# First two blocks of an attention and MLP kernel: scores from keys in place, value tiles loaded, weights decoded in four single steps, a new prologue order

## The chip, the cores and the metric

The kernel runs on one core of one Trainium2 chip. The metric is the device time of one execution in microseconds (us). Five engines work side by side, each with its own queue in order: TensorE (PE; its weight loads are listed as PEld), VectorE (DVE), ScalarE (ACT), GpSimd (POOL) and SyncE (SP), which issues all transfers here.

## The reference

`B, H, S, D = 4, 8, 768, 64`; the model width is 512, the MLP width 1536.

```python
k_sum = k.reshape(B, H, nb, block, D).max(axis=3)      # block = 32
v_sum = v.reshape(B, H, nb, block, D).mean(axis=3)
mask_l = np.abs(pos[:, None] - pos[None, :]) < window  # window = 16
scores_l = scale * q @ k^T, -1e9 outside mask_l
scores_s = scale * q @ k_sum^T + log(block)
a = softmax(concat([scores_l, scores_s]))
x = a @ concat([v, v_sum])                             # then heads side by side
g = x @ w_gate;  out = (silu(g) * (x @ w_val)) @ w_out
```

Each position sees its neighbours within 16 and 24 pooled blocks. The MLP weights arrive as float64.

## The kernel before

The 3072 tokens are 8 blocks of 384, two per batch. A block's attention runs by four pairs of heads u; a pair has 128 partitions (two heads of 64). Queries come in six tiles of 64; a tile's keys are a window of 96 and 24 pooled ones, so a score row has 120 columns. The MLP runs by 12 steps j of 128 hidden units; every product is made of three in a short float format, from a high and a low part of each operand. A step of one block is three groups on PE: gate (12 matmuls), val (12) and down (9 of 512 columns, accumulated in three banks over all j).

Every weight is decoded once on the chip, from the two 32-bit words of a float64: ACT takes the absolute value of the high word into a tile `m` (`w_abs`); DVE clamps it (L183), shifts it (L185), sets sign and top bits (L193) and the bits of the low word (L196); a cast makes the high part (`w_hi`, L152 on DVE or L150 on ACT) and a subtraction the low part (`w_lo`, L146 on DVE or POOL). Gate and value weights of steps 1 to 10 go together as `gv` (1024 columns, "wide"), those of steps 0 and 11 and all output weights `o` have 512 ("narrow"). Step 11 is loaded only when the pool `dec`, which holds the `m` tiles of `gv`, is closed (`room(1)`).

The first two blocks (k = 0 and 1) are a prologue: a hand-held table, `PROLOGUE`, lists every step in the order in which it is issued, with the engine behind `=` (`a` ACT, `d` DVE, `p` POOL) where there is a choice. Each engine keeps that order. The table ends with block 0 complete and with steps 0 to 5 of block 1: 18 steps, 54 groups. From there a loop issues the rest of the MLP, with the attention of later blocks between. Names of the table: `kt` and `q` load keys and queries; `winA`, `winB`, `join` put block 0's windows together out of `kt` and the pooled keys; `kw` loads windows for block 1; `pool` makes the pooled keys; `scores`; `ttr` adds bias and takes the maximum; `exp`; `rcp` the reciprocal of the sum; `nrm` multiplies by it; `tr` and `pt` transpose and copy from PSUM; `out` multiplies by the values; `split` and `rest` make high and low part of x; `silu`, `mul`, `ah`, `al` make the high and low part of the MLP's middle. Argument pairs are (block, pair) up to `rest` and (block, step) behind it.

Block 0's values: `vn` loads value rows in tiles of 128 starting at 0, from which windows of even query tiles are read in place; `odd1`, `odd2` copy odd windows out of it, `first_values` sums blocks on PE, `fv_copy`, `val1`, `val2` copy these sums behind each window. Block 1's windows are loaded by `vw` and completed by `values`.

SP issues in order and has eight transfer semaphores, so an issue waits for the eighth before it.

Of the kernel before, what the change touches and what calls it, by code (L numbers as in the profile page):

```python
# [72 lines left out]
fv_copy(0)=a nrm(0,1)=d tr0(0,3) pt1(0,3)=a w_load(1,gv) pt0(0,3)=a val1(0,1)=d tr1(0,1) val2(0,1)=a pool(2)
join(0,0)=p tr0(0,1) val1(0,2)=p pt1(0,1)=a out(0,3) winB(0)=p w_abs(0,g) winA(2)=d join(0,2)=d pt0(0,1)=a
w_clamp(0,g) val1(0,0)=a out(0,1) vw(1,0) split(0,3)=a w_bits(0,g) winB(2)=a vw(1,1) val2(0,0)=a scores(1,0)
split(0,1)=a rest(0,3) q(0,0) rest(0,1) w_abs(1,gv) w_load(0,v) w_hi(0,g)=d ttr0(1,0) w_lo(0,g)=p values(1,0)=a
ttr1(1,0) w_load(2,o) exp0(1,0) values(1,1)=p scores(0,0) w_clamp(1,gv) w_load(0,o) exp1(1,0) ttr0(0,0)
w_abs(0,v) w_load(1,o) rcp(1,0) exp0(0,0) ttr1(0,0) nrm(1,0)=p q(0,2) exp1(0,0) w_load(3,o) w_clamp(0,v)
tr1(1,0) tr0(1,0) pt1(1,0)=a rcp(0,0) scores(1,1) w_bits(0,v) w_abs(2,o) w_load(2,gv) w_abs(1,o) scores(0,2)
ttr0(1,1) nrm(0,0)=p w_abs(0,o) pt0(1,0)=a ttr1(1,1) exp0(1,1) out(1,0) w_clamp(1,o) kw(1,3) w_clamp(0,o)  # L80
tr0(0,0) exp1(1,1) tr1(0,0) ttr0(0,2) kw(1,2) pt1(0,0)=a rcp(1,1) q(1,2) split(1,0)=a ttr1(0,2) nrm(1,1)=p
pt0(0,0)=a vw(1,2) rest(1,0) exp0(0,2) out(0,0) w_load(4,gv) w_bits(0,o) exp1(0,2) tr0(1,1) tr1(1,1) join(1,2)=d
w_hi(0,v)=d join(1,3)=a scores(1,2) rcp(0,2) pt0(1,1)=a values(1,2)=d pt1(1,1)=a nrm(0,2)=d w_load(5,gv)
w_hi(0,o)=a out(1,1) split(0,0)=a w_bits(1,o) tr1(0,2) split(1,1)=a tr0(0,2) pt1(0,2)=a rest(0,0) w_lo(0,v)=p
pt0(0,2)=a ttr0(1,2) w_hi(1,o)=a out(0,2) vw(1,3) rest(1,1) w_lo(0,o)=p exp0(1,2) ttr1(1,2) q(1,3) split(0,2)=d
room(0) w_load(7,gv) exp1(1,2) w_lo(1,o)=p rest(0,2) gate(0,0) rcp(1,2) values(1,3)=d nrm(1,2)=d val(0,0)
silu(0,0) w_bits(1,gv) w_load(6,gv) tr1(1,2) tr0(1,2) pt1(1,2)=a scores(1,3) w_clamp(2,o) w_hi(1,gv)=a
w_load(9,o) mul(0,0) pt0(1,2)=a w_lo(1,gv)=p ttr0(1,3) ah(0,0)=a out(1,2) ttr1(1,3) exp0(1,3) w_load(8,o)
split(1,2)=d rest(1,2) w_load(7,o) gate(0,1) w_bits(2,o) exp1(1,3) w_load(9,gv) al(0,0)=d w_abs(2,gv) rcp(1,3)
val(0,1) nrm(1,3)=d silu(0,1) w_clamp(2,gv) w_load(8,gv) tr1(1,3) w_bits(2,gv) tr0(1,3) w_abs(6,gv) down(0,0)  # L90
pt1(1,3)=a pt0(1,3)=a w_hi(2,o)=a w_clamp(6,gv) out(1,3) w_load(6,o) w_hi(2,gv)=a mul(0,1) w_lo(2,gv)=p
split(1,3)=a w_load(3,gv) ah(0,1)=a rest(1,3) gate(1,0) val(1,0) silu(1,0) al(0,1)=d w_abs(4,gv) w_bits(6,gv)
w_load(10,o) down(0,1) w_load(5,o) mul(1,0) w_lo(2,o)=d ah(1,0)=a w_load(10,gv) al(1,0)=d gate(1,1) w_abs(7,o)
w_hi(6,gv)=d w_abs(3,o) w_clamp(7,o) w_abs(6,o) w_clamp(3,o) val(1,1) silu(1,1) w_bits(7,o) w_load(4,o)
w_lo(6,gv)=d w_hi(7,o)=a down(1,0) w_clamp(6,o) w_abs(3,gv) mul(1,1) w_lo(7,o)=p ah(1,1)=a gate(0,2) al(1,1)=d
w_abs(4,o) w_clamp(3,gv) w_bits(6,o) val(0,2) silu(0,2) w_bits(3,gv) w_hi(6,o)=a down(1,1) mul(0,2) w_hi(3,gv)=d
gate(1,2) ah(0,2)=d w_lo(3,gv)=d al(0,2)=d val(1,2) w_lo(6,o)=d silu(1,2) w_clamp(4,o) w_bits(3,o) down(0,2)
mul(1,2) w_hi(3,o)=a w_clamp(4,gv) ah(1,2)=a gate(0,3) al(1,2)=d w_bits(4,gv) val(0,3) silu(0,3) w_bits(4,o)
w_hi(4,gv)=d w_hi(4,o)=a down(1,2) mul(0,3) w_lo(3,o)=p ah(0,3)=d w_abs(8,o) w_lo(4,gv)=d gate(1,3) w_abs(9,o)
al(0,3)=d w_abs(7,gv) w_clamp(9,o) w_abs(5,gv) w_clamp(8,o) val(1,3) w_bits(9,o) silu(1,3) w_clamp(5,gv)  # L100
down(0,3) mul(1,3) w_clamp(7,gv) ah(1,3)=a gate(0,4) al(1,3)=d w_bits(7,gv) val(0,4) silu(0,4) w_bits(8,o)
down(1,3) mul(0,4) w_hi(8,o)=a w_hi(7,gv)=d ah(0,4)=a w_lo(4,o)=d al(0,4)=d w_abs(10,o) gate(1,4) w_bits(5,gv)
val(1,4) silu(1,4) w_clamp(10,o) w_hi(5,gv)=d w_bits(10,o) down(0,4) w_lo(5,gv)=d w_hi(10,o)=d gate(0,5)
mul(1,4) w_lo(8,o)=p ah(1,4)=a al(1,4)=d w_abs(5,o) w_hi(9,o)=d val(0,5) w_clamp(5,o) silu(0,5) w_lo(10,o)=p
w_bits(5,o) down(1,4) mul(0,5) w_lo(9,o)=p gate(1,5) w_hi(5,o)=d ah(0,5)=d w_lo(5,o)=d al(0,5)=d w_lo(7,gv)=p
val(1,5) silu(1,5) down(0,5) mul(1,5) w_abs(8,gv) ah(1,5)=a w_clamp(8,gv) w_abs(10,gv) gate(0,6) al(1,5)=d
w_bits(8,gv) val(0,6) silu(0,6) w_clamp(10,gv) down(1,5) w_hi(8,gv)=d w_bits(10,gv) gate(0,7) mul(0,6)
w_lo(8,gv)=p ah(0,6)=a val(0,7) silu(0,7) al(0,6)=d w_abs(9,gv) w_hi(10,gv)=d down(0,6) mul(0,7) w_clamp(9,gv)
ah(0,7)=d w_lo(10,gv)=d gate(0,8) al(0,7)=d w_bits(9,gv) val(0,8) silu(0,8) w_hi(9,gv)=d down(0,7) mul(0,8)
w_lo(9,gv)=d ah(0,8)=a al(0,8)=p room(1) w_load(11,g) gate(0,9) w_load(11,v) val(0,9) silu(0,9) w_load(11,o)  # L110
w_abs(11,g) w_clamp(11,g) down(0,8) mul(0,9) w_abs(11,v) w_bits(11,g) ah(0,9)=a w_abs(11,o) gate(0,10) al(0,9)=d
w_hi(11,g)=d w_clamp(11,o) w_clamp(11,v) val(0,10) silu(0,10) w_bits(11,o) w_bits(11,v) w_hi(11,o)=a down(0,9)
# [13 lines left out]
def body(ctx, tc, qP, kP, vT, vP, wgv, wo, bias, ident, mean, out):  # L126
# [51 lines left out]
    def w_clamp(j, nm):  # L178

        low, high, m = W[nm, j]  # L180
        f = m.bitcast(I32)

        nc.vector.tensor_scalar(out=m, in0=m, scalar1=F64_LO, scalar2=F64_HI, op0=ALU.max, op1=ALU.min)  # L183

        nc.vector.tensor_scalar(  # L185
            out=f, in0=f, scalar1=3, scalar2=0x3FFFFFF8,
            op0=ALU.logical_shift_left, op1=ALU.bitwise_and,
        )

    def w_bits(j, nm):  # L190
        low, high, m = W[nm, j]
        f = m.bitcast(I32)
        nc.vector.scalar_tensor_tensor(  # L193
            out=f, in0=high, scalar=-0x40000000, in1=f, op0=ALU.bitwise_and, op1=ALU.bitwise_or
        )
        nc.vector.scalar_tensor_tensor(  # L196
            out=f, in0=low, scalar=29, in1=f, op0=ALU.logical_shift_right, op1=ALU.bitwise_or
        )
# [531 lines left out]
```

## Time and profile before

| | |
|---|---|
| median of 3 runs | 736.31 us (736.21 to 736.46) |
| span of the profiled execution | 735.9 us, the profiled execution's own time by its records |
| PE busy | 707.3 us (96%), 4958 matmuls |
| DVE busy | 302.2 us (41%) |
| ACT busy | 310.3 us (42%) |
| POOL busy | 156.6 us (21%) |
| moved by DMA | 62.02 MB, mean 84 GB/s |

The shares are means over two unlike stages: the prologue, in which attention and all weights are prepared, and the long stage behind it. A profile row gives start, duration, engine, line, operation, output and inputs; a bracket gives the idle time ahead and what ended it. A group row gives busy time and mean duration of one in ns.

### The profile page before, as it was taken

The numbers are of one execution on the slowest core, as the hardware profiler recorded it, in microseconds if no ns is written. First come the engines' busy times: TensorE is split into PE (matmuls) and PEld (weight loads), VectorE is DVE, ScalarE is ACT, GpSimd is POOL, SyncE is SP. The second block draws the span as 40 slices with busy tenths as digits, with TensorE's granted clock in tenths as the row PEclk, the third lists the DMA queues.
The fourth block names the chain that finished last, engine by engine and source line by source line (L and its number), as shares of the span: only waits on it lengthen the run. The fifth ranks groups of instructions, "written<-read, shape, count | busy, mean of one in ns | idle before, by whom it ended". The sixth has DMA issues, their size and how long they took to land.

```text
span 735.9 us, 12480 instructions
## 1 busy us (share of the span) xinstructions
PE 707.3 (96%) x4958; PEld 643.5 (87%) x4958; DVE 302.2 (41%) x833; ACT 310.3 (42%) x772; POOL 156.6 (21%) x161
## 2 busy tenths in 40 slices
...
GB/s 311 320 307 413 94 1 0 1 73 97 208 155 167 65 44 45 30 79 65 69 85 87 109 38 7 44 86 44 44 44 44 54 33 17 1 14 31 1 0 44
DMA packets 56666, 62.02 MB, mean 84 GB/s; under 512 B 24288, under 2 KB 46752, under 8 KB 55328
## 3 DMA queue, kind: packets, MB, share of 16 engines
...
## 4 chain that ended last, share of the span: by engine, by line
PE 80%; DVE 10%; issue 3%; ACT 3%; DMA 2%; POOL 1%; SPq 0%; DVEq 0%; POOLq 0%; ACTq 0%
PE v L494 24%; PE g L494 24%; PE acc L545 23%; PE xo L468 3%; PE sc L378 3%; PE pp L444 2%; DVE m_gv L193 1%; DMA stg<-in_kP 1%; PE pv L359 1%; ACT p L408 1%; DVE w_gv L146 1%; DVE a L506 1%; DVE m_gv L196 1%; DMA bias_sb<-in_bias 1%; DVE m_gv L185 1%
## 5 line engine op out<-in xcount | busy, mean ns | idle before, releaser
L494 PE MATMUL g<-xh,w_gv 128*128 128x384 f32 x640 | 179.8, 342 | 5.6 <-DVE w_gv L146 4.4
L494 PE MATMUL v<-xh,w_gv 128*128 128x384 f32 x640 | 180.0, 342 | 1.4 <-DVE a L506 1.4
L545 PE MATMUL acc<-w_o,ah 128*128 128x512 f32 x576 | 179.2, 392 | 0.0
L506 DVE TENSOR_TENSOR a<-v,a 128x384 f32<-128x384 f32 x96 | 53.4, 556 | 248.7 <-PE v L494 248.0
L146 POOL TENSOR_TENSOR al<-a,ah 128x384 fp32r<-128x384 f32 x79 | 80.7, 1022 | 270.2 <-ACT ah L150 260.1
L494 PEld LDWEIGHTS g<-xh,w_gv 128*128 128x128 f32 x640 | 118.4, 190 | 9.0 <-issue 4.4
L545 PEld LDWEIGHTS acc<-w_o,ah 128*128 128x128 f32 x576 | 108.0, 188 | 20.2
L494 PEld LDWEIGHTS v<-xh,w_gv 128*128 128x128 f32 x640 | 117.9, 189 | 5.0 <-issue 2.4
L545 PE MATMUL acc<-w_o,al 128*128 128x512 f32 x288 | 114.1, 396 | 0.1
L501 ACT ACTIVATE a<-g 128x384 f32<-128x384 f32 x96 | 47.2, 492 | 156.5 <-PE g L494 152.5
L494 PE MATMUL g<-xl,w_gv 128*128 128x384 f32 x320 | 108.8, 340 | 0.0
L494 PE MATMUL v<-xl,w_gv 128*128 128x384 f32 x320 | 108.1, 338 | 0.0
L150 ACT CAST ah<-a 128x384 fp32r<-128x384 f32 x91 | 46.4, 510 | 126.0 <-DVE a L506 126.0
L408 ACT ACTIVATE p<-p,nm 128x120 f32<-128x120 f32 x192 | 73.2, 383 | 2.5 <-DVE nm L393 2.1
L545 PEld LDWEIGHTS acc<-w_o,al 128*128 128x128 f32 x288 | 54.0, 188 | 10.2 <-issue 0.6
L494 PEld LDWEIGHTS g<-xl,w_gv 128*128 128x128 f32 x320 | 60.7, 190 | 2.5
L494 PEld LDWEIGHTS v<-xl,w_gv 128*128 128x128 f32 x320 | 60.5, 189 | 0.0
L430 POOL TENSOR_TENSOR p<-p,ri 128x720 f32<-128x720 f32 x27 | 37.8, 1401 | 101.8 <-DVE ri L426 95.7
L501 ACT ACT_TABLE_LOAD x26 | 33.4, 1283 | 52.3 <-PE g L494 52.2
L393 DVE CUSTOM_DVE_ANT_0 p<-sc,bias_sb 128x120 f32<-128x120 f32 x192 | 41.4, 276 | 2.2 <-PE sc L378 2.0
L494 PE MATMUL g<-xh,w_g 128*128 128x384 f32 x128 | 37.5, 355 | 0.0
L494 PE MATMUL v<-xh,w_v 128*128 128x384 f32 x128 | 36.3, 344 | 0.0
...
## 6 DMA issues: line engine op xcount, KB each, us to landing
...
kw<-in_kP SPq DMA_DIRECT2D x28, 288.0 KB, 4.0
vw<-in_vP SPq DMA_DIRECT2D x28, 288.0 KB, 3.3
...
out<-o SPq DMA_DIRECT2D x23, 256.0 KB, 2.3
...
```

Of the source, the lines that this page charges most:

```text
L146: (nc.vector if e == "d" else nc.gpsimd).tensor_tensor(out=out, in0=a, in1=b.bitcast(F32), op=ALU.subtract)
L150: nc.scalar.copy(out, in_)
L378: nc.tensor.matmul(sc[h][s * QT : (s + 1) * QT, c * KC : (c + 1) * KC], t["q"][hs, qs], t["kw"][hs, i, :], start=True, stop=True,)
L393: nc.vector.tensor_tensor_reduce(out=t["p"][:, i, :], in0=t["sc"][g][:, c * KC : (c + 1) * KC], in1=bias_sb[:, 0 if n == 0 else 2 if n == ...
L408: nc.scalar.activation(out=t["p"][:, i, :], in_=t["p"][:, i, :], func=AF.Exp, scale=-1.0, bias=t["nm"][:, i : i + 1], accum_out=t["sm"][:, ...
L430: (nc.vector if on == "d" else nc.gpsimd).tensor_tensor(out=p, in0=p, in1=ri.rearrange("p (n o) -> p n o", o=1).broadcast_to([P, NT, KC]), ...
L444: nc.tensor.transpose(ps[:KC, c * P : (c + 1) * P], U[k, u]["p"][:, g * NT // 2 + c, :], id_sb)
L468: nc.tensor.matmul(ps[hs, qs], vw, t["pt"][:, h, qs], start=True, stop=True)
L494: nc.tensor.matmul(ps[:, :TOK], w[:, cs], x, start=u == 0 and n == 0, stop=u == NP - 1 and n == 2)
L501: nc.scalar.activation(out=a, in_=A.pop(("g", k, j))[:, :TOK], func=AF.Silu)
L506: nc.vector.tensor_tensor(out=a, in0=ps[:, :TOK], in1=a, op=ALU.mult)
L545: nc.tensor.matmul(ACC[k][i], a[:, ts], w, start=j == 0 and n == 0, stop=j == NJ - 1 and n == 2)
```

## The change

Scores of blocks 0 and 1 are made in two parts: `sw` multiplies a query tile with 96 columns of the key tile in place, `sp` with the 24 pooled keys. No windows are copied, joined or loaded in these blocks. Even and odd value windows of both blocks come from two tiles, `vn` (all four pairs, loaded by `vn` and `vr`) and `vo` (loaded by `vo`, from row 64 on). The block sums of all pairs land in one bank (`fv`), four copies move them out (`fvc`), and two transfers from on-chip memory to on-chip memory spread them behind all even and all odd windows (`spn`, `spo`). The decoding steps of a weight, `w_clamp` (two instructions) and `w_bits` (two), become `w_c1`, `w_c2`, `w_s1`, `w_s2`, each with its own place in the table. PSUM banks are named in the table (`g`, `a`, `b`). Gate and val of step 0 can be issued by pair (`gate(0,0,2)`). The table is new as a whole.

```diff
+    def a_score_part(k, u, keys, cols):
+        t = U[k, u]
+        for i in range(NT):
+            c, s = divmod(i, 2)
+            qs = slice(i * QT, (i + 1) * QT)
+            for h in range(2):
+                hs = slice(h * D, (h + 1) * D)
+                nc.tensor.matmul(
+                    t["sc"][h][s * QT : (s + 1) * QT, c * KC + cols[0] : c * KC + cols[1]], t["q"][hs, qs],
+                    keys(hs, i), start=True, stop=True,
+                )
+    def a_near(k, u):
+        U[k, u]["sc"] = [a_bank(k, u, f"sc{h}", on[h]) for h in range(2)]
+        a = k % HALVES * TOK
+        a_score_part(k, u, lambda hs, i: KT[u][hs, a + i * QT : a + i * QT + KW], (0, KW))
+    def a_far(k, u):
+        a_score_part(k, u, lambda hs, i: ksum[u][hs, :], (KW, KC))
...
+    def v_sums():
+        vn["sums"] = ps = a_bank(0, 0, "pv", on)
+        for i in range(NV):
+            for u in range(NP):
+                nc.tensor.matmul(
+                    ps[u * QC : (u + 1) * QC, :P], mean_sb[:, i, :], vn["even"][:, i, u * P : (u + 1) * P],
+                    start=i == 0, stop=i == NV - 1,
+                )
+    def v_keep():
+        vsum["all"] = one.tile([KC, DM], F32, tag="vs", name="vs_0")
+        ps = vn.pop("sums")
+        for u in range(NP):
+            copy(on, vsum["all"][KW:, u * P : (u + 1) * P], ps[u * QC : u * QC + NB, :P])
+    def v_spread(x):
+        src = vsum["all"][KW:].rearrange("n (o d) -> n o d", o=1).broadcast_to([NB, ODD, DM])
+        nc.sync.dma_start(vn[x][KW:KC, :ODD], src)
...
-                if k:
-                    vw = t["vw"][:, i, hs]
-                else:
-                    vw = t["vw"][:, i // 2, hs] if i % 2 else t["vn"][:KC, i // 2, hs]
+                if k < HALVES:
+                    w = k * NT + i
+                    vw = vn["odd" if w % 2 else "even"][:KC, w // 2, u * P + h * D : u * P + (h + 1) * D]
...
-q(0,3) kt(3) kt(1) q(0,1) mean() bias() pool(3) winB(3)=p vn(2) winA(3)=p join(0,3)=a winA(1)=d winB(1)=a
+kt(0) q(0,0) pool(0) bias() sw(0,0)=ag sp(0,0) q(1,0) ttr0(0,0) mean() sw(1,0)=aa sp(1,0) kt(1) ttr1(0,0)
```

POOL, from the first wide subtraction on, before (`w_gv1` is the pair of tiles of step 1; `al_0_8` belongs to block 0, step 8):

```order
L146 TENSOR_TENSOR w_gv1_753<-m_gv1_354,w_gv1_753 128x1024
L146 TENSOR_TENSOR w_gv2_888<-m_gv2_818,w_gv2_888 128x1024
L146 TENSOR_TENSOR w_o7_1000<-m_o7_968,w_o7_1000 128x512
L146 TENSOR_TENSOR w_o3_1122<-m_o3_972,w_o3_1122 128x512
L146 TENSOR_TENSOR w_o8_1284<-m_o8_1179,w_o8_1284 128x512
L146 TENSOR_TENSOR w_o10_1341<-m_o10_1293,w_o10_1341 128x512
L146 TENSOR_TENSOR w_o9_1364<-m_o9_1195,w_o9_1364 128x512
L146 TENSOR_TENSOR w_gv7_1286<-m_gv7_1199,w_gv7_1286 128x1024
L146 TENSOR_TENSOR w_gv8_1494<-m_gv8_1443,w_gv8_1494 128x1024
L146 TENSOR_TENSOR al_0_8_1598<-a_0_8_1581,ah_0_8_1596 128x384
```

and after, from the first MLP step on:

```order
L147 TENSOR_TENSOR al_0_0_856<-a_0_0_832,ah_0_0_854 128x384
L147 TENSOR_TENSOR w_o0_849<-m_o0_717,w_o0_849 128x512
L147 TENSOR_TENSOR al_1_0_954<-a_1_0_893,ah_1_0_946 128x384
L147 TENSOR_TENSOR al_0_1_1015<-a_0_1_959,ah_0_1_998 128x384
L147 TENSOR_TENSOR al_1_1_1068<-a_1_1_961,ah_1_1_1066 128x384
L147 TENSOR_TENSOR w_gv3_1116<-m_gv3_951,w_gv3_1116 128x1024
L147 TENSOR_TENSOR w_gv5_1108<-m_gv5_1033,w_gv5_1108 128x1024
L147 TENSOR_TENSOR w_o3_1178<-m_o3_1090,w_o3_1178 128x512
L147 TENSOR_TENSOR al_1_2_1220<-a_1_2_1071,ah_1_2_1161 128x384
L147 TENSOR_TENSOR w_gv4_1217<-m_gv4_1156,w_gv4_1217 128x1024
```

The subtractions `al`, which stood on DVE before, now stand on POOL between the weights, and six wide `w_lo` are there instead of four.

DVE, in the middle of the weights, before:

```order
L183 TENSOR_SCALAR m_o7_968<-m_o7_968 128x512
L185 TENSOR_SCALAR m_o7_968<-m_o7_968 128x512
L183 TENSOR_SCALAR m_o3_972<-m_o3_972 128x512
L185 TENSOR_SCALAR m_o3_972<-m_o3_972 128x512
L193 SCALAR_TENSOR_TENSOR m_o7_968<-raw_o7_794,m_o7_968 128x512
L196 SCALAR_TENSOR_TENSOR m_o7_968<-raw_o7_794,m_o7_968 128x512
L146 TENSOR_TENSOR w_gv6_970<-m_gv6_852,w_gv6_970 128x1024
```

and after, at the weights of steps 3 to 5:

```order
L185 TENSOR_SCALAR m_gv3_951<-m_gv3_951 128x1024
L147 TENSOR_TENSOR w_o1_996<-m_o1_779,w_o1_996 128x512
L181 TENSOR_SCALAR m_gv5_1033<-m_gv5_1033 128x1024
L185 TENSOR_SCALAR m_gv5_1033<-m_gv5_1033 128x1024
L193 SCALAR_TENSOR_TENSOR m_gv5_1033<-raw_gv5_798,m_gv5_1033 128x1024
L193 SCALAR_TENSOR_TENSOR m_gv3_951<-raw_gv3_928,m_gv3_951 128x1024
L200 SCALAR_TENSOR_TENSOR m_gv3_951<-raw_gv3_928,m_gv3_951 128x1024
L181 TENSOR_SCALAR m_o3_1090<-m_o3_1090 128x512
```

The two instructions of a clamp or of the bits always stood next to each other; now other tiles' steps often stand between.

SP, where the values are loaded, before:

```order
L587 DMA vn2_121<-in_vP 128x6x256
L588 DMA vn2_121<-in_vP 32x256
L587 DMA vn0_146<-in_vP 128x6x256
L588 DMA vn0_146<-in_vP 32x256
L246 DMA kw_1_1_193<-in_kP 128x6x96
```

and after, with the ACT rows on which the spreading transfers wait:

```order
L577 DMA vn_219<-in_vP 128x6x512
L167 DMA raw_v0_373<-in_wgv 128x1024
L587 DMA vo_430<-in_vP 96x3x512 x2
L236 DMA q_1_3_521<-in_qP 128x384
L332 DMA vn_219<-vs_0_491 24x6x512
L332 DMA vo_430<-vs_0_491 24x6x512
L167 DMA raw_o0_584<-in_wo 128x1024
L167 DMA raw_gv1_641<-in_wgv 128x2048
```

```order
L393 ACTIVATE p_0_3_289,sm_0_3_291<-p_0_3_289,nm_0_3_290 128x120 x3
L176 ACTIVATE m_v0_446<-raw_v0_373 128x512
L151 COPY vs_0_491<-pv_0_0_449 24x128 x4
L393 ACTIVATE p_0_3_289,sm_0_3_291<-p_0_3_289,nm_0_3_290 128x120 x3
L393 ACTIVATE p_0_2_419,sm_0_2_421<-p_0_2_419,nm_0_2_420 128x120 x6
```

Two large value loads were among the first ten transfers and nothing on SP waited for an engine there; now one load of all pairs comes as the seventeenth, two transfers behind it wait for the copies of the sums on ACT, and all weights but step 0's gate and value are behind these two.

More of the change, by code (lines that the diff above doesn't have):

```diff
@@ L73 @@
[L73 to L112, printed above, removed]
@@ L113 @@
-mul(0,10) w_lo(11,g)=p w_hi(11,v)=a ah(0,10)=d w_lo(11,v)=d load(2,0) gate(0,11) w_lo(11,o)=d al(0,10)=p
-val(0,11) silu(0,11) down(0,10) mul(0,11) ah(0,11)=a al(0,11)=d down(0,11)
+kt(0) q(0,0) pool(0) bias() sw(0,0)=ag sp(0,0) q(1,0) ttr0(0,0) mean() sw(1,0)=aa sp(1,0) kt(1) ttr1(0,0)
+pool(1) q(0,1) exp0(0,0) ttr0(1,0) kt(3) exp1(0,0) sw(0,1)=bg q(1,1) ttr1(1,0) vr() pool(3) sp(0,1) q(0,3)
+sw(0,3)=ag w_load(0,g) exp0(1,0) rcp(0,0) kt(2) id() exp1(1,0) ttr0(0,1) ttr1(0,1) sp(0,3) nrm(0,0)=p ttr0(0,3)
@@ new lines @@
+w_c2(0,v) pt0(0,1)=d w_hi(0,g)=d rcp(0,2) nrm(0,3)=p spo() sw(1,3)=ab tr0(1,1)=b tr1(1,1)=b pt1(0,1)=d sp(1,3)
+ttr0(1,3) ttr1(1,3) w_load(0,o) exp0(1,2) tr0(0,3)=g nrm(0,2)=p out(1,0)=a exp1(1,2) out(0,0)=g tr1(0,3)=a
+pt0(1,1)=d pt1(1,1)=a split(1,0)=a pt0(0,3)=a tr0(0,2)=a rcp(1,2) w_load(1,gv) rest(1,0) split(0,0)=a exp0(1,3)
+w_s1(0,v) rest(0,0) w_lo(0,g)=p nrm(1,2)=p out(0,1)=b w_load(3,o) pt1(0,3)=a tr1(0,2)=b pt0(0,2)=d pt1(0,2)=a
+w_s2(0,v) out(1,1)=b split(0,1)=a tr0(1,2)=a gate(0,0,0) exp1(1,3) pt0(1,2)=d w_hi(0,v)=d w_load(1,o) tr1(1,2)=a
@@ new lines @@
+rest(0,1) pt1(1,2)=a w_abs(0,o) w_lo(0,v)=d out(0,3)=a split(1,1)=a rcp(1,3) split(0,3)=d out(0,2)=a
+split(0,2)=a out(1,2)=a rest(1,1) rest(0,2) rest(0,3) w_c1(0,o) w_c2(0,o) val(0,0,0) w_abs(1,o) gate(0,0,1)
+gate(0,0,2) nrm(1,3)=p w_abs(1,gv) tr0(1,3)=a tr1(1,3)=b w_load(5,gv) gate(0,0,3) pt0(1,3)=a val(0,0,1)
+val(0,0,2) pt1(1,3)=a out(1,3)=a val(0,0,3) split(1,2)=a w_c1(1,gv) silu(0,0) w_c1(1,o) w_c2(1,gv) w_s1(0,o)
+w_s2(0,o) rest(1,2) w_load(2,gv) w_load(2,o) w_load(4,o) mul(0,0) split(1,3)=a w_hi(0,o)=a rest(1,3)
@@ new lines @@
+w_load(4,gv) ah(0,0)=a al(0,0)=p w_s1(1,gv) w_s2(1,gv) gate(1,0) room(0) w_c2(1,o) w_abs(2,gv) val(1,0)
+silu(1,0) mul(1,0) w_abs(2,o) w_lo(0,o)=p down(0,0) w_hi(1,gv)=a w_lo(1,gv)=d gate(0,1) w_c1(2,gv) w_load(3,gv)
+gate(1,1) w_load(8,gv) w_c1(2,o) ah(1,0)=d w_abs(4,o) w_c2(2,gv) w_abs(3,gv) w_c1(3,gv) al(1,0)=p w_c2(2,o)
+w_s1(2,o) w_s1(2,gv) silu(0,1) silu(1,1) w_s2(2,o) w_s2(2,gv) val(0,1) val(1,1) w_s1(1,o) w_hi(2,gv)=d mul(0,1)
+w_s2(1,o) w_hi(1,o)=a ah(0,1)=d w_lo(2,gv)=d mul(1,1) down(1,0) w_c1(4,o) al(0,1)=p w_c2(4,o) gate(0,2)
@@ new lines @@
+w_load(9,gv) w_abs(5,gv) gate(1,2) w_c2(3,gv) w_load(7,gv) silu(0,2) val(0,2) ah(1,1)=a al(1,1)=p w_lo(1,o)=d
+silu(1,2) w_c1(5,gv) w_c2(5,gv) w_s1(5,gv) val(1,2) w_s1(3,gv) w_abs(3,o) w_hi(2,o)=a w_s2(3,gv) w_c1(3,o)
+w_s1(4,o) mul(1,2) down(0,1) w_s2(5,gv) w_hi(5,gv)=d mul(0,2) ah(0,2)=d al(0,2)=d w_lo(2,o)=d w_hi(3,gv)=a
+w_lo(3,gv)=p w_load(6,o) down(1,1) gate(0,3) val(0,3) w_abs(4,gv) w_c2(3,o) w_load(10,o) ah(1,2)=a w_abs(6,o)
+w_s1(3,o) w_s2(3,o) w_lo(5,gv)=p w_s2(4,o) w_load(6,gv) w_c1(4,gv) w_abs(7,gv) w_load(8,o) w_load(5,o)
@@ new lines @@
+w_hi(3,o)=a w_c2(4,gv) down(0,2) w_s1(4,gv) w_s2(4,gv) silu(0,3) mul(0,3) ah(0,3)=a w_load(9,o) w_c1(6,o)
+w_load(10,gv) w_c1(7,gv) gate(1,3) w_lo(3,o)=p w_hi(4,gv)=d w_c2(6,o) al(1,2)=p w_hi(4,o)=a w_s1(6,o) w_c2(7,gv)
+al(0,3)=d w_s2(6,o) w_s1(7,gv) w_lo(4,gv)=p w_s2(7,gv) w_lo(4,o)=p silu(1,3) down(1,2) w_abs(5,o) val(1,3)
+mul(1,3) w_hi(7,gv)=d w_abs(10,o) w_c1(5,o) ah(1,3)=a gate(1,4) silu(1,4) gate(0,4) w_abs(6,gv) al(1,3)=p
+w_c1(6,gv) w_c2(5,o) silu(0,4) w_c1(10,o) val(0,4) val(1,4) w_c2(6,gv) w_s1(5,o) w_c2(10,o) w_s2(5,o) down(0,3)
```

176 lines of the change are left out of this document (84 added, 92 removed).

## The prediction

> **What bounds the kernel now.** I read first the busy time by stretch, then the waits of TensorE (PE), then the rows of the first 182 us on each engine. By stretch, here PE (three rows), VectorE (DVE, two) and GpSimd (POOL, two); columns are stretch, length, busy time, count, granted clock, DMA share and GB/s:
>
> ```profile
> 0.00:56.00 56.00, 39.08 (x422) 0.85 0.93 314
> 56.00:160.00 104.00, 96.91 (x548) 0.97 0.25 87
> 182.00:735.90 553.90, 549.70 (x3880) 1.00 0.20 59
> ...
> 0.00:56.00 56.00, 45.26 (x150) 0.85 0.93 314
> 56.00:160.00 104.00, 94.37 (x143) 0.97 0.25 87
> ...
> 0.00:56.00 56.00, 17.11 (x24) 0.85 0.93 314
> 56.00:160.00 104.00, 17.77 (x10) 0.97 0.25 87
> ```
>
> Behind 182 us PE is full and nothing is changed, so the change can only move the moment at which the first two blocks end. The marks on PE: first product of the MLP, its waits, and the last product of block 0.
>
> ```profile
> 49.61 0.69 PE L494 MATMUL g<-xh,w_g 128*128 128x384 f32 x1
> 60.60 0.44 PE L494 MATMUL g<-xh,w_gv 128*128 128x384 f32 x1 [1.14 <-POOL w_gv L146]
> 125.25 0.41 PE L494 MATMUL g<-xh,w_gv 128*128 128x384 f32 x1 [4.00 <-DVE w_gv L146]
> 160.43 0.41 PE L494 MATMUL g<-xh,w_gv 128*128 128x384 f32 x1 [0.41 <-DVE w_gv L146]
> 180.90 0.61 PE L545 MATMUL acc<-w_o,ah 128*128 128x512 f32 x2
> ```
>
> From 160.43 to 181.51 stand ten groups (gate, val or down of one step), 2.11 us each. The prologue holds 18 steps, 54 groups, 114 us; from 49.61 that would end at 163.5 instead of 181.5. The waits named at PE's rows are for weights (`w_gv`), from DVE or from POOL, which gets them from DVE, and DVE, which makes them, is busy 94.37 of 104 us. So the bound of this stage is DVE: its last weight of steps 0 to 10 is subtracted at
>
> ```profile
> 159.07 1.22 DVE L146 TENSOR_TENSOR w_gv<-m_gv,w_gv 128x1024 fp32r<-128x1024 f32 x1
> 163.88 0.43 DVE L183 TENSOR_SCALAR m_g<-m_g 128x512 f32<-128x512 f32 x1 [3.60 <-ACT m_g L175]
> ```
>
> and ends at 160.3; 21.2 us later the prologue is over. I therefore work out when this point comes after the change, and what follows it.
>
> **Prices on DVE.** What an instruction costs a full engine is the distance of two starts:
>
> ```profile
> 63.88 0.69 DVE L183 TENSOR_SCALAR m_gv<-m_gv 128x1024 f32<-128x1024 f32 x1
> 64.60 0.69 DVE L185 TENSOR_SCALAR m_gv<-m_gv 128x1024 int32<-128x1024 int32 x1
> 65.33 1.23 DVE L193 SCALAR_TENSOR_TENSOR m_gv<-raw_gv,m_gv 128x1024 int32<-128x1024 int32 x1
> 66.59 1.22 DVE L196 SCALAR_TENSOR_TENSOR m_gv<-raw_gv,m_gv 128x1024 int32<-128x1024 int32 x1
> 67.73 0.69 DVE L183 TENSOR_SCALAR m_gv<-m_gv 128x1024 f32<-128x1024 f32 x1
> ...
> 68.45 0.69 DVE L185 TENSOR_SCALAR m_gv<-m_gv 128x1024 int32<-128x1024 int32 x1
> 69.06 0.55 DVE L506 TENSOR_TENSOR a<-v,a 128x384 f32<-128x384 f32 x1
> ```
>
> A step followed by the next step on the same tile takes 0.72; followed by other work 0.61 (68.45 to 69.06). So a dependent neighbour costs 0.11, and a duration is about 0.08 more than its slot.
>
> 1. *Instructions off and on DVE.* The groups of the first 160 us (`pt` from behind 182):
>
> ```profile
> L430 DVE TENSOR_TENSOR p<-p,ri 128x720 f32<-128x720 f32 x5 | 5.5, 1097 | 0.2
> L146 DVE TENSOR_TENSOR al<-a,ah 128x384 fp32r<-128x384 f32 x14 | 8.4, 598 | 1.7 <-ACT ah L150 1.7
> L152 DVE COPY vw<-vs 24x768 f32<-24x768 f32 x2 | 2.0, 1000 | 0.1
> ...
> L152 DVE COPY pt<-pp 120x384 f32<-120x384 f32 x24 | 13.4, 556 | 36.0 <-PE pp L444 36.0
> ```
>
> In DVE's order go: 5 `nrm` (5.5), 10 of 16 `al` (6.0), 13 copies for windows and values (the two largest are the 2.0 above; the rest at about 0.35, so 5.9), 2 `w_lo` of both halves (1.22 each, 2.4), and one wide and one narrow `w_hi` and one `split`, under 0.7 each (1.7): 21.5. There come 8 `pt` (4.4), 2 `ah` and one narrow `w_lo` (1.4): 5.8. Net 15.7, less 0.08 for each of 22 instructions: 14 us off; since `nrm`, copies and `al` in these means were partly held up by POOL, I take 13.
>
> 2. *Four single steps.* In before 52 pairs (L183 and L185, L193 and L196) stand next to each other on one tile. In after 19 do, and 5 more places put other steps of one tile side by side, so 28 dependences are gone: 28 x 0.11 = 3 us off. The steps' number and work are unchanged.
>
> 3. *Order.* Behind the last wide weight after has about 3 us more to do than before (two `mul`, the end of `w_o7`): 3 us off this point, paid in the tail.
>
> 4. *POOL.* Its work grows: `nrm` from 3 to 8, `al` from 2 to 12, wide `w_lo` from 4 to 6, against one narrow `w_lo` and 13 small copies. What that costs DVE:
>
> ```profile
> L430 POOL TENSOR_TENSOR p<-p,ri 128x720 f32<-128x720 f32 x24 | 33.4, 1391 | 94.4 <-DVE ri L426 94.4
> L146 POOL TENSOR_TENSOR al<-a,ah 128x384 fp32r<-128x384 f32 x77 | 78.1, 1014 | 253.4 <-ACT ah L150 248.0 <-DMA vt<-in_vT 5.4
> ...
> 127.69 1.39 POOL L146 TENSOR_TENSOR w_o<-m_o,w_o 128x512 fp32r<-128x512 f32 x1 [0.83 <-DVE w_o L152]
> 129.04 2.58 POOL L146 TENSOR_TENSOR w_gv<-m_gv,w_gv 128x1024 fp32r<-128x1024 f32 x1
> 129.40 2.77 DVE L193 SCALAR_TENSOR_TENSOR m_o<-raw_o,m_o 128x512 int32<-128x512 int32 x1
> 132.21 0.69 DVE L196 SCALAR_TENSOR_TENSOR m_o<-raw_o,m_o 128x512 int32<-128x512 int32 x1
> ...
> 58.18 2.36 POOL L146 TENSOR_TENSOR w_gv<-m_gv,w_gv 128x1024 fp32r<-128x1024 f32 x1 [8.23 <-ACT w_gv L150]
> 59.51 0.56 DVE L152 CAST xh<-xo 128x384 fp32r<-128x384 f32 x1
> ```
>
> The step at 129.40 takes 2.77 instead of 0.69: it ends 0.55 after POOL does. The one at 59.51, which reads PSUM, is not delayed beside the same POOL work. Added by slots, the 143 instructions of 56 to 160 cost 85; the stretch has 94.37, so POOL's 17.77 us cost 9, half. In after POOL does in that stage 9 `al` (9.1), 6 wide (14.2) and 7 narrow `w_lo` (9.5): 33 us, at half 17, 8 more. Ahead of it: before lost 45.26 - 40 = 5; after has there 8 `nrm` and one `w_lo`, 12 us, mostly beside work from PSUM: 3. Together 6 us on. The bounds are 0 (all of it beside PSUM work or waits) and 33 - 9 = 24 (all of it paid).
>
> The Trainium skill, "SBUF — State Buffer", section "Who interferes with whom", says that the two share a port pair under an exclusive lock, and that the loser is blocked for the whole instruction when VectorE has two SBUF inputs or a two-port mode. By that rule alone the 24 would be the price, and the sum below would be 18 us more. The trace agrees at 129.40 and finds half over the stage, since part of POOL's work falls into DVE's waits.
>
> 5. *The way to the first product.* Prices:
>
> ```profile
> 5.21 0.95 DVE L275 TENSOR_REDUCE ks<-kt 128x24 f32<-128x768 f32 x1 [4.21 <-DMA kt<-in_kP]
> ...
> L408 ACT ACTIVATE p<-p,nm 128x120 f32<-128x120 f32 x48 | 18.3, 383 | 1.7 <-DVE nm L393 1.6
> L359 PE MATMUL pv<-vn,mean_sb 128*24 128x256 f32 x24 | 6.7, 439 | 0.6 <-DVE nm L393 0.6
> ...
> kw<-in_kP SPq DMA_DIRECT2D x28, 288.0 KB, 4.0
> out<-o SPq DMA_DIRECT2D x23, 256.0 KB, 2.3
> ```
>
> After begins with the same 592 KB, so DVE at 5.2. `vn` (all even value tiles) closes 5.4 MB; at 314 GB/s 17.2 us, landed at 20. The block sums stream as many columns as before (28 x 128 for 14 x 256), 7 us: 27. Four copies on ScalarE (ACT): 28.2. The two spreading transfers follow (between 2.3 and 4.0, I take 3.3, the kind is not in the trace): 31.5, where `out(1,0)` can start. On ACT the copies stand ahead of the last exponentials of (0,3) and all of (0,2), (1,2): three at 0.38 make 29.4, and until then DVE, done at 24.5, waits at `rcp(0,3)`: 5 us. From there ACT sets the pace, at 0.38 for an exponential and under 0.5 for a copy: exponentials of (0,2) to 31.7, of (1,2) to 34.0, a `pt`, a `split`, a `pt`, `split(0,0)` at 35.7; DVE's `rest(0,0)` at 36.4. PE has by then three `out` and the transposes between them and begins `gate(0,0,0)` at 37. DVE goes on with two steps of `w_v0`, two `pt`, `w_hi`, a `rest` and `w_lo`, to 39.6, where `val(0,0,0)` may begin. The last pair (1,3) hangs on `rcp(1,3)` at 40: `nrm` 41.4, transposes 43, `pt` on ACT 43.7, `out` 46, `split` 46.5, `rest` 48. The wide weight of step 1 stands behind it on DVE: `w_lo(1,gv)` ends at 52.4, when PE has done both blocks' step 0 and `down(0,0)`. The estimate for any of these is good to some 3 us. DVE's slots up to there add to 38, so start and waits are 14.5, against 10.7 in before's first 56 us. The two-part scores add 12 short matmuls of 24 columns to each of eight score steps; between nothing and a doubling of before's score rows that is 0 to 1 us a step, in a stage where PE is busy 39 of 56 us; I take half, hidden, because DVE and ACT pace the stage. SP's queue stands still from `q(1,3)` to 28; behind the spread come `w_o0` (wanted on ACT at 40) and `w_gv1` (42), landing before 36: covered by 5 us, and without that cover each us late is one us on PE.
>
> In the stage after it before waited 104 - 94.37 = 9.6; after stands shorter, I take 7.5. Waits together: 22 against 20.3, 2 on. The nearest rows are before's own, so the ends are 14 and 32.
>
> **The sum.** -13 - 3 - 3 + 6 + 2 = -11: the last wide weight is ready at 149.3. The tail grows: step 11 loads only when the decoding pool is free (as at 163.88, 3.6 us later), DVE's order puts eight more instructions into `w_lo(11,g)`, 12 us after the point, and six groups of 2.11 follow: 24.6 instead of 21.2. The prologue ends at 173.9, 7.6 us earlier. The profiled span is 735.9, the median 736.31, 0.4 above; 736.3 - 7.6 gives about 728.
>
> **Rivals.**
> - *PE becomes the bound.* If POOL costs little, only PE's own work is left: at 52.4 five groups are done, 49 remain at 2.11, so 156, with 3 us of waits 159. For it: 49.61 to 181.51 holds 18 us of loss. Against it: PE would then want the point at 134.5 (eleven groups follow `w_gv9`, which ends 1.7 ahead of it); DVE has 69 us of slots from 52.4, so it is there at 122 with no wait and no lock, and at 134 only with half of the 17 and half of the 7.5. The prologue ends 22 us earlier: 714.
> - *The lock takes it all (other side).* DVE is so dense that nothing of POOL's work falls into waits. Price 18 above my sum, deciding from 7.6: slower if POOL's cost passes three quarters of its busy time. At nine tenths, 740. For it: 129.40; against: the half measured over 104 us. The skill's rule above would give this.
> - *The value path is late.* Vector waits pass one to one into the point. If `vn` lands at 24 and the transfers take 4, DVE waits 8 more: 736, no change.
>
> **How the numbers follow.** Forecast (720 to 734.8) 0.60; PE-bound or nearly, below 720, 0.13; no change (within 0.2%, 1.5 us, what a measurement can tell here) 0.10; slower by the lock 0.11, by waits 0.06. Faster 0.73, same 0.10, slower 0.17. The range leaves out the outer half of the PE case and the slow end: 716 to 738.5.
>
> **What would show it.** In after: DVE's last wide `w_gv` at 149 (143 to 156); first gate near 37 and `w_gv1` at 52; ACT idle ahead of the four `vs` copies; DVE busy in the weight stage still over 90%, with steps of 2 to 3 us beside wide POOL ones; span behind the last `down` of block 0 still 554. Wrong would be PE waits under 8 us behind 52 (PE bound), or DVE held up over 25 us by POOL.

## The result, and the profile after

The changed kernel takes 731.42 us (median of 4 runs, 730.91 to 732.35), the kernel before 736.35 beside it: a ratio of 0.9935, with a 95% interval of 0.9921 to 0.9949. It is faster by 0.65%, 4.9 us, where 8.3 were forecast. Measured again beside the experiments it took 731.18 (6 runs), ratio 0.9940 (0.9924 to 0.9956). Its profiled execution spans 729.9 us and took 731.64.

Busy time by stretch of the changed kernel, TensorE (PE, three rows), VectorE (DVE, two) and GpSimd (POOL, two), in the columns of the prediction's first fence:

```profile
0.00:56.00 56.00, 43.23 (x763) 0.91 0.97 333
56.00:160.00 104.00, 93.61 (x465) 0.97 0.28 94
174.15:729.90 555.75, 551.88 (x3882) 1.00 0.20 59
...
0.00:56.00 56.00, 42.28 (x160) 0.91 0.97 333
56.00:160.00 104.00, 96.68 (x125) 0.97 0.28 94
...
0.00:56.00 56.00, 17.44 (x16) 0.91 0.97 333
56.00:160.00 104.00, 38.15 (x21) 0.97 0.28 94
```

VectorE is fuller still in the weight stage (96.68 of 104 us), and GpSimd works 38.15 us there instead of 17.77. The marks: first gate, last wide weight, `w_lo(11,g)`, and the copy of block 0's first result, with which the first two blocks end:

```profile
39.05 0.42 PE L482 MATMUL g<-xh,w_g 128*128 128x384 f32 x1
...
148.16 1.23 DVE L147 TENSOR_TENSOR w_gv<-m_gv,w_gv 128x1024 fp32r<-128x1024 f32 x1
...
159.81 0.69 DVE L147 TENSOR_TENSOR w_g<-m_g,w_g 128x512 fp32r<-128x512 f32 x1 [0.41 <-ACT w_g L151]
...
173.46 0.69 DVE L153 COPY o<-acc 128x512 f32<-128x512 f32 x1 [1.82 <-PE acc L532]
```

The last wide weight is ready at 149.39 (149.3 forecast), 10.9 us ahead of before's 160.29. The same copy stood in before at 180.87, so the first two blocks are 7.4 us shorter (7.6 forecast). Yet the span is only 6.0 us shorter: behind them the changed kernel takes 555.75 us, 1.4 more than before's 554.4 from 181.5, in code that was not changed.

### The profile page after: what moved, and what is told of

It is laid out like the page before. It is cut to its first block, busy times and chain, and to the rows that moved or that the text cites. A ratio compares the mean times of both kernels' runs of the same rounds, so it can differ in the third digit from the quotient of the medians.

```text
span 729.9 us, 12894 instructions
## 1 busy us (share of the span) xinstructions
PE 702.9 (96%) x5178; PEld 643.3 (88%) x5178; DVE 295.3 (40%) x812; ACT 300.8 (41%) x754; POOL 177.3 (24%) x165
## 4 chain that ended last, share of the span: by engine, by line
PE 84%; DVE 9%; DMA 3%; issue 2%; ACT 1%; SPq 0%; DVEq 0%; ACTq 0%
PE v L482 25%; PE g L482 25%; PE acc L532 24%; PE xo L454 4%; PE pp L429 3%; DMA q<-in_qP 2%; PE sc L343 2%; DVE m_gv L193 2%; DVE m_gv L200 1%; DMA kt<-in_kP 1%; DVE a L493 1%; DVE m_gv L181 1%; DVE m_o L193 1%; DVE m_gv L185 1%; DVE w_gv L147 0%
## 5 line engine op out<-in xcount | busy, mean ns | idle before, releaser
L147 POOL TENSOR_TENSOR al<-a,ah 128x384 fp32r<-128x384 f32 x89 | 95.4, 1072 | 300.3 <-ACT ah L151 272.2
L415 POOL TENSOR_TENSOR p<-p,ri 128x720 f32<-128x720 f32 x32 | 44.8, 1401 | 124.3 <-DVE ri L411 108.0
```

Source lines behind the costliest of these rows:

```text
L147: (nc.vector if e == "d" else nc.gpsimd).tensor_tensor(out=out, in0=a, in1=b.bitcast(F32), op=ALU.subtract)
L415: (nc.vector if on == "d" else nc.gpsimd).tensor_tensor(out=p, in0=p, in1=ri.rearrange("p (n o) -> p n o", o=1).broadcast_to([P, NT, KC]), ...
```

## Experiments

Medians are given beside each experiment's ratio to the kernel before on its own chip. What a time contains is read from profiles, mark by mark.

**The queries of (1,3).** In the start the chain that holds up the first gate is not the one that the prediction named. Rows of the changed kernel: the block sums, the scores of (1,3), the first products of values (PE), the copies of the pooled values (ScalarE, ACT) and VectorE behind the scores:

```profile
20.50 1.74 PE L317 MATMUL pv<-vn,mean_sb 128*32 128x128 f32 x56 [2.50 <-DVE m_g L193]
28.30 1.24 PE L356 MATMUL sc<-kt,q 64*64 64x96 f32 x24 [4.79 <-DMA q<-in_qP]
32.55 0.48 PE L454 MATMUL xo<-pt,vn 120*64 120x64 f32 x4
...
22.92 1.06 ACT L151 COPY vs<-pv 24x128 f32<-24x128 f32 x4
...
31.95 0.28 DVE L378 CUSTOM_DVE_ANT_0 p<-sc,bias_sb 128x120 f32<-128x120 f32 x1 [3.57 <-PE sc L356]
```

The sums were done at 22.2, not 27, but PE stood 4.79 us and VectorE 3.57 us until `q(1,3)` had landed, the last of the first loads. The edit:

```diff
-... q(1,2) vn() w_c1(0,g) ... ttr1(1,2) q(1,3) exp1(0,2) ...
+... q(1,2) q(1,3) vn() w_c1(0,g) ... ttr1(1,2) exp1(0,2) ...
```

> The load q(1,3) is moved ahead of the even value tiles on SP's queue; nothing else changes. Theory (in the changed kernel the queries q(1,3) land last and hold up TensorE 4.79 us and, behind it, VectorE 3.6 us at 28 us): the row sc<-kt,q of (1,3) waits under 1 us, the first gate comes at 36 to 37 instead of 39.05, the last wide weight is ready 2 to 4 us ahead of 149.4, and the time is 728.4 (727.4 to 729.6). Rival (something else paces the stage, the pooled values that the two transfers bring at 32, or ScalarE's exponentials, so the wait moves by a few rows only): the first gate stays within 0.7 us and the time within 0.7 us of 731.4.

Measured: 733.0 us, ratio 0.9959 (0.9946 to 0.9972). PE's rows at the same place:

```profile
24.72 0.73 PE L356 MATMUL sc<-kt,q 64*64 64x96 f32 x24
...
30.60 0.48 PE L454 MATMUL xo<-pt,vn 120*64 120x64 f32 x4 [0.67 <-DMA vn<-vs]
33.71 0.48 PE L454 MATMUL xo<-pt,vo 120*64 120x64 f32 x4 [2.63 <-DMA vo<-vs]
...
39.72 0.42 PE L482 MATMUL g<-xh,w_g 128*128 128x384 f32 x1
```

The wait for the queries is gone, and the same time is spent one row later on the second spreading transfer. The changed kernel itself, profiled a second time, waits 2.22 us for the queries and then for that transfer as well:

```profile
33.55 0.34 PE L454 MATMUL xo<-pt,vo 120*64 120x64 f32 x4 [1.24 <-DMA vo<-vs]
```

So two chains end within about a microsecond of each other there, and taking one away brings nothing: the first gate stayed within 0.7 us, as the rival has it. The time did not: it is 1.6 us above 731.4, and with intervals that overlap a little the record does not show whether the edit costs something. The weight `v` of step 0 now lands later, its abs stands ahead of the four copies on ScalarE, and so the copies moved from 22.92 to 25.02.

**The pooled values earlier.** The edit takes both chains forward:

```diff
-... vn() w_c1(0,g) ... w_load(0,v) ... vo(1) ... w_abs(0,v) ... fvc()=a w_c1(0,v) ... q(1,3) ... w_c2(0,v) ... exp1(1,2) ...
+... vn() q(1,3) w_c1(0,g) ... vo(1) w_load(0,v) ... fvc()=a ... exp1(1,2) w_abs(0,v) w_c1(0,v) w_c2(0,v) ...
```

> In the changed kernel q(1,3) is loaded right behind the even value tiles, the first narrow weight v of step 0 behind the odd ones, and its abs on ScalarE and first two steps on VectorE stand behind the exponentials of (1,2), so that the four copies of the pooled values on ScalarE no longer wait for that weight. Theory (the pooled values' way, sums, four copies, two transfers, paces the stage once q(1,3) is early): copies at 22.3 to 23.3, transfers issued at 23.3 and 24.3, first product of pooled values at 30 to 31.3 instead of 32.55, first gate 1 to 2.5 us ahead of 39.05, last wide weight as much ahead of 149.4, time 729.5 (728.5 to 730.7). Rival (the two steps that VectorE now does later cost there what is won): first gate earlier, last wide weight and time within 0.5 us.

In the profile the first product of pooled values came at 29.53, the first gate at 38.09 and the last wide weight at 148.43, close to what the theory has. The time did not follow: 732.71 us (12 runs, 730.39 to 735.03), ratio 0.9961 (0.9947 to 0.9975). One profile was no evidence here: over the eight profiles whose instructions up to the first gate are the changed kernel's own (the kernel twice, and the six experiments below that edit only later work or places), the first gate lies anywhere between 37.52 and 40.11 us. The loads are not all that differs there: the mean granted clock of TensorE up to the first gate was 0.91 in the profile with the earliest gate, 0.79 in the one with the latest and 0.82 to 0.87 in the others; how much of the scatter comes from it was not tested. A gain of 1 us in the start is within that scatter, so whether this edit brings anything is not settled; nothing in the times speaks for it.

**GpSimd's price.** From the start of `w_lo(1,gv)` to the last wide weight the stage repeats well (95.40 and 95.11 us in the changed kernel's two profiles), so it is what I compare. Two experiments change GpSimd's work.

```diff
-al(k,j)=p   (12 of them in the table)
+al(k,j)=d
```

> The 12 subtractions al that the changed kernel does on GpSimd inside the first two blocks are done on VectorE. VectorE's own work grows by 4.0 us up to the last wide weight and 5.3 us up to the end of the first two blocks; GpSimd loses about 12 us. If GpSimd's work costs VectorE half of its busy time (the forecast's price), the two cancel: within 1.5 us of 731.4. If it costs all of it, 6 us faster (725.5). If it costs nothing, 4 to 5 us slower (736).

```diff
     def m_low(k, j):
         ah, a = A[k, j]
+        if on == "p":
+            A[k, j] = (ah, ah)
+            return
```

> The 12 subtractions al that the changed kernel does on GpSimd inside the first two blocks are left out, and TensorE reads ah in their place (so the low part of these activations is missing from the result); VectorE's instructions are unchanged. If GpSimd's work costs VectorE half of its busy time: last wide weight 4.5 us ahead of 149.4, time 726 (725 to 727.5). If it costs all: 9 to 12 us, 721. If it costs nothing, or if TensorE and not VectorE bounds the stage: within 1 us of 731.4.

Measured: `al` on VectorE 732.28 us (0.9951, 0.9937 to 0.9965); without `al` 726.19 (0.9874, 0.9852 to 0.9896). Busy time of that stage, VectorE and then GpSimd, of the changed kernel, with `al` on VectorE, and without these `al`:

```profile
53.99:149.39 95.40, 88.63 (x109) 0.96 0.26 90
53.99:149.39 95.40, 37.08 (x20) 0.96 0.26 90
```

```profile
54.96:150.33 95.37, 89.46 (x116) 0.93 0.27 93
54.96:150.33 95.37, 25.97 (x12) 0.93 0.27 93
```

```profile
52.87:144.40 91.53, 83.16 (x108) 0.96 0.28 99
52.87:144.40 91.53, 24.39 (x12) 0.96 0.28 99
```

By the prediction's slots the changed kernel's 107 VectorE instructions of the stage cost 70.4 us. VectorE was busy 88.63, so 18.2 us were spent in instructions that took longer beside GpSimd: 0.49 of GpSimd's 37.08. With `al` on VectorE the slots are 73.9, the excess 15.5 of 25.97 (0.60); without `al` it is 12.8 of 24.39 (0.52). Of the 12.7 us that GpSimd was spared in the last case, VectorE's excess lost 5.4, and 1.6 of these came back as waits, so the stage is 3.9 shorter; another 1.1 lies ahead of it, within the scatter of the start. Half of GpSimd's busy time was the forecast's price, and both times came out as that price has them. The Trainium skill, "SBUF — State Buffer", section "Who interferes with whom", has the two engines under an exclusive lock. The trace agrees that one holds the other up, but over the stage VectorE paid half of GpSimd's time, not all: the full price would have made the run without `al` 721 us.

**Single steps next to each other again.**

```diff
-w_c1(j,x) ... w_c2(j,x) ... w_s1(j,x) ... w_s2(j,x)
+w_c1(j,x) w_c2(j,x) ... w_s1(j,x) w_s2(j,x)      (the first moved down to the second)
```

> In the order of the first two blocks each first step (range, top bits) stands directly ahead of the second step on the same tile (shift, rest) again, as in the kernel before. 27 more instructions of VectorE then read what the instruction just before them wrote, up to the last wide weight, 32 up to the end. Theory (0.11 us each): last wide weight 3.0 us later than 149.4, time 734.7 (733.5 to 736). Rival (what such a pair costs is hidden in waits or beside GpSimd's work): within 0.7 us of 731.4.

Measured: 735.92 us (12 runs, 732.39 to 737.75), ratio 0.9989 (0.9974 to 1.0004), nearly all of the gain gone. The last wide weight came at 153.87, 4.5 later; 1.7 of that is a later start of the stage (55.66, for 52.48 to 54.96 in the runs with the changed kernel's start; the edit moves steps there too), and the rest is the stage itself:

```profile
55.66:153.87 98.21, 92.76 (x109) 0.97 0.24 81
```

It is 2.8 us longer than 95.40. In the stage 22 more instructions read what the one ahead of them wrote, 0.13 us each, against 0.11 in the prediction. The single steps are worth 3 us, as forecast.

**Is VectorE the bound?** One instruction per wide weight is left out.

```diff
     def w_top(j, nm):
+        if nm == "gv":
+            return
```

> In the changed kernel the third of the four weight steps (sign and top exponent bit, 1.14 us each on VectorE) is left out for the ten wide weights, so these weights are wrong; nothing else changes. If VectorE bounds the first two blocks to their end: last wide weight 11 us ahead of 149.4, the blocks' end 11 us ahead of 174, time 721 (720 to 723). If TensorE is the bound, or nearly: TensorE's waits behind 55 us cannot fall below zero, so at most 8 of the 11 come through and the time stays above 723.5.

Measured: 720.74 us, ratio 0.9805 (0.9787 to 0.9824), last wide weight at 137.41, copy of the first result at 161.46, both 12.0 us earlier. The stage starts 2.5 us earlier, 1.1 for the first of the instructions left out and the rest within the scatter of the start.

```profile
51.46:137.41 85.95, 75.82 (x100) 1.00 0.32 114
```

The nine of these instructions that fall into the stage have slots of 10.3 us, and it is 9.45 shorter. What VectorE is spared arrives at the end almost in full: the rival that PE takes over is out, for another 10 us at least. Not for much more: PE was busy 82.12 of the 85.95 us here.

**Rounding on ScalarE.** The same without leaving work out:

```diff
-w_hi(2,gv)=d w_hi(4,gv)=d w_hi(5,gv)=d w_hi(7,gv)=d w_hi(8,gv)=d w_hi(9,gv)=d
+w_hi(2,gv)=a w_hi(4,gv)=a w_hi(5,gv)=a w_hi(7,gv)=a w_hi(8,gv)=a w_hi(9,gv)=a
```

> Six of the wide roundings w_hi (steps 2, 4, 5, 7, 8, 9) go from VectorE to ScalarE, which is busy 31.68 of 104 us there. VectorE has 6 x 0.60 = 3.6 us less to do before the last wide weight. Theory (VectorE is the bound and ScalarE has room): last wide weight 3 to 3.6 us earlier, time 728 (727.5 to 729). Rival (the round trip through ScalarE takes the place: VectorE or GpSimd waits for the rounding ahead of the subtraction): within 1 us of 731.4, or slower.

Measured: 729.95 us, ratio 0.9918 (0.9903 to 0.9933), last wide weight at 147.09.

```profile
53.87:147.09 93.22, 85.95 (x103) 0.96 0.28 99
```

The stage is 2.2 us shorter for 3.7 us of slots: 1.1 went into a larger excess beside GpSimd (19.3 for 18.2) and 0.5 into waits. The time lies between the two expectations.

**Both.** The rounding on ScalarE and the earlier pooled values together:

> Both edits that brought the last wide weight forward are joined: the six wide roundings on ScalarE (149.4 to 147.1 in the profile) and the earlier pooled values (149.4 to 148.4). If VectorE's chain passes both on one to one: last wide weight at 146 (145.3 to 146.7), time 727.5 (726.5 to 728.8). If the earlier values only move the wait, as the median of the runs with that edit alone (732.7) hints: within 0.7 us of 730.

Measured: 730.6 us, ratio 0.9929 (0.9912 to 0.9945), first gate at 39.44, last wide weight at 147.06. The earlier values added nothing to the rounding, so the second expectation holds.

**The 1.4 us behind the first two blocks.** The kernel before was profiled again, and the changed kernel too:

> The kernel before, profiled on the same chip as these runs. The span behind the last down of block 0 was 555.0 us in the profile shown and 556.4 in each profile since (after and four experiments). If the change or its order costs 1.4 us there, this run shows 555.0 again; if the profiles were taken on chips whose clocks differ by 0.25%, it shows 556.4, and the time lies 1.8 us above the span as in the experiments, not 0.4.

> The changed kernel again, on the chip of these runs, to be compared with its variants there. Time 731.4 (730.9 to 732.4), 0.9935 of the kernel before; stretch behind the last down of block 0 556.4 us.

Span and clock, and the copy of block 0's first result; the kernel before, then the changed one:

```profile
core 0: 734.4 us, clock 0.984
179.64 0.69 DVE L152 COPY o<-acc 128x512 f32<-128x512 f32 x1 [1.73 <-PE acc L545]
```

```profile
core 0: 728.8 us, clock 0.988
172.36 0.69 DVE L153 COPY o<-acc 128x512 f32<-128x512 f32 x1 [1.81 <-PE acc L532]
226.32 0.69 DVE L153 COPY o<-acc 128x512 f32<-128x512 f32 x1 [1.02 <-PE acc L532]
311.71 0.69 DVE L153 COPY o<-acc 128x512 f32<-128x512 f32 x1 [0.73 <-PE acc L532]
```

The run of the kernel before took 736.22 us, 1.8 above its span like every run of the changed kernel: that the first profile's span lay only 0.4 under the median of the kernel before has nothing to do with the change. But from the copy to the end it took 554.8 us again, and the changed kernel 556.4. Neither clause of the expectation holds alone: the 1.3 us by which 0.4 differs from 1.8 are not the change's, the 1.7 us behind the copy are. They come evenly: block 2 (copy to copy) takes 311.71 - 226.32 = 85.39 us, and in the first profile of the kernel before

```profile
234.96 0.69 DVE L152 COPY o<-acc 128x512 f32<-128x512 f32 x1 [1.01 <-PE acc L545]
320.10 0.69 DVE L152 COPY o<-acc 128x512 f32<-128x512 f32 x1 [0.73 <-PE acc L545]
```

85.14. PE waits for nothing in either; its products are a little slower. The same 28 us of the second half of block 2, the kernel before and the changed one:

```profile
L494 PE MATMUL g<-xh,w_gv 128*128 128x384 f32 x32 | 8.9, 338 | 0.0
```

```profile
L482 PE MATMUL g<-xh,w_gv 128*128 128x384 f32 x32 | 9.0, 340 | 0.0
```

What differs for these instructions is where their tiles lie: a pool hands out places in the order in which its tiles are first used, and the new table changed that order for the weights and for the pool of `xh`, `xl`, `q`, `kw`, `vw` and `p`. The experiment asks the pools for the places of the kernel before, by naming the tiles in its order ahead of the table (abridged):

```diff
+    place(att, 2, kw q vw xh3 xl3 xh1 xl1 p xh0 xl0 xh2 xl2)
+    place(wts[0], 1, g0 gv1 v0 o2 o0 o1 o3 gv2 gv4 gv5 gv3 o5 o4)
...
             wts.append(pool("wts2", 1, reuse_waits="tile"))
+            place(wts[1], 1, gv7 gv6 o9 o8 o7 gv9 gv8 o6 o10 gv10)
```

> The changed kernel with its weights and the activations xh, xl at the places in SBUF that they have in the kernel before (the pools give places in the order of first use, and the new table uses them in another order); the instructions and their order are the changed kernel's. The stretch behind the last down of block 0 took 554.8 and 555.0 us in two profiles of the kernel before and 556.4 to 557.0 in the eight of the changed table, with the same instructions there. If the places cost it: 555.0 here, and the time 730.0. If they do not: 556.4, time 731.4 (some loads may wait longer for room in the first blocks, up to 1 us more).

Measured: 729.77 us, ratio 0.9917 (0.9899 to 0.9935).

```profile
core 0: 726.4 us, clock 0.988
171.74 0.69 DVE L153 COPY o<-acc 128x512 f32<-128x512 f32 x1 [1.80 <-PE acc L532]
225.50 0.69 DVE L153 COPY o<-acc 128x512 f32<-128x512 f32 x1 [1.01 <-PE acc L532]
310.63 0.69 DVE L153 COPY o<-acc 128x512 f32<-128x512 f32 x1 [0.73 <-PE acc L532]
```

554.7 us behind the copy, 85.13 for block 2: the changed kernel's instructions in the old places lose nothing. All 26 weights, `xh`, `xl`, `kw`, `vw` and `p` lie where the kernel before has them; `pt`, `ah`, `o` and other tiles whose places differ between the two kernels keep the changed kernel's, so those cost nothing here. Then with the weights alone in their old places, and the rounding on ScalarE (against the edit above):

```diff
-    place(att, 2, ...)
+    w_hi of steps 2, 4, 5, 7, 8, 9: =a
```

> The changed kernel with the six wide roundings on ScalarE and with the 26 weights at the places in SBUF that they have in the kernel before; xh and xl stay at the changed kernel's places. The stretch behind the last down of block 0 took 554.7 us with all places as before and 556.4 with the changed kernel's. If the weights' places cost the 1.7 us: 554.7 again, and with the roundings' 2.3 us in the first blocks the time is 728 (727 to 729). If the places of xh and xl cost it: 556.4, and the time is 729.8 (729 to 730.6).

Measured: 729.02 us, ratio 0.9912 (0.9898 to 0.9927).

```profile
core 0: 725.5 us, clock 0.990
169.09 0.69 DVE L153 COPY o<-acc 128x512 f32<-128x512 f32 x1 [1.79 <-PE acc L532]
```

556.4 us behind the copy: the weights' places alone do not bring it back. So it is the places of the other pool's tiles, or those together with the weights'; which tile it is, and why, stays open. Of the kernels that do the whole work this one has the lowest time, 2.2 us under the changed kernel's 731.18, with intervals that overlap a little. The rounding on ScalarE with all the old places was not run.

## Why the prediction was right in its direction and 3.4 us too hopeful

- *DVE bounds the stage.* Shown by leaving one instruction per wide weight out: 9.45 of 10.3 us came through the stage, and the whole 12.0 us earlier last weight reached the end.
- *Instructions off VectorE (-13), single steps (-3), order (-3), POOL (+6), waits (+2): last wide weight at 149.3.* It was ready at 149.39, and the parts agree as well. Up to that point the prediction has 38 + 69 us of slots, 3 + 17 beside POOL and 14.5 + 7.5 of start and waits (start, then weight stage); with its 38 us of slots, measured were 38 + 69.3, 3.5 + 18.2 and 13.7 + 6.8. The weight stage was sized to within 1 us. Its walk through the start, though, puts the end of `w_lo(1,gv)` at 52.4, and it came at 55.2: 52.4 holds the 38 and the 14.5 alone, and the 3 us beside POOL, which the sum charges, are missing in it.
- *Single steps.* 3 us forecast, 2.8 lost in the stage when they were put back.
- *POOL at half.* GpSimd worked 37 to 38 us in the stage, not 33, because its own narrow `w_lo` and `al` were held up as well (1.83 us each instead of 1.42 in the kernel before, and 1.49 instead of 1.02 behind the first two blocks); the share was 0.49, and between 0.45 and 0.60 in the five experiments whose slots I added.
- *The way to the first product.* The mechanism was wrong in two places. The block sums took 1.74 us, not 7: 56 product records of 128 columns into 32-column outputs, four outputs side by side, so a quarter of the 7 us. And what arrived late was `q(1,3)` on SP's queue; VectorE waited 0.69 us at `rcp(0,3)`, not 5, and 3.57 at the scores of (1,3). The two errors partly cancel: first gate 39.05 for 37. The rival "the value path is late" did not decide.
- *The tail.* 24.6 us forecast from the last wide weight to the end of the first two blocks, 24.8 measured; `w_lo(11,g)` ended 11.1 us behind the point, for 12.
- *"Behind 182 us PE is full and nothing is changed, so the change can only move the moment at which the first two blocks end."* This step failed. The instructions were the same and their tiles' places were not: 1.4 us in the first pair of profiles, 1.7 to 1.8 in the later ones, shown by putting the tiles back.
- *From the span to the time.* The prediction put 0.4 us between them, from the first profile's span and the median of other runs. In every run of which the record has both, the time is 1.7 to 1.9 us above the span. So that profile was of an execution of about 737.7 us (an estimate, 735.9 + 1.8), 1.3 above the median. In the second profile, of a run of 736.22, the same copy stands at 179.64 instead of 180.87: nearly all of the 1.3 us lies in the first two blocks, and the forecast started from a slow sample of them.
- *"736.3 - 7.6 gives about 728."* It gives 728.7; 0.7 of the 3.4 us is this step.
- So the profiles shown have 7.4 us won in the first two blocks and 1.4 given back behind them, 6.0 of span. Between the medians it is 4.9 us: an estimated 6.3 to 6.6 won in the first two blocks, less the 1.4 to 1.7 behind them. That 149.39 lies so near 149.3 is in part luck: in the second profile of the kernel before the last wide weight is ready at 159.07, from where the same 11 us would have given 148.1.
